# Transposing W2 by DMA instead of on TensorE, with another order of loads and of the first item's work

## The chip, the core and the metric

The kernel runs on one core of one Trainium2 chip. A core has TensorE (PE: matrix products and their weight loads, PEld), VectorE (DVE), ScalarE (ACT), GpSimd (POOL) and SyncE (SP); each runs its own instructions in order. Sixteen DMA engines, which all queues share, move data between HBM (the chip's main memory) and SBUF (the on-chip working memory), and inside SBUF. TensorE writes to PSUM, the accumulator memory, from which VectorE or ScalarE copy to SBUF. The metric is device time in microseconds (us), the median of several runs.

## What is computed

Block-sorted attention with a Sinkhorn-normalised permutation, followed by a layer that takes the larger of two products:

```python
for _ in range(5):                       # P = sort_net, (4 items, 8 heads, 8, 8)
    P = exp(P - max(P)); P = P / sum(P, -1); P = P / sum(P, -2)
k_sorted = einsum('bhij,bhjcd->bhicd', P, k_blocks)      # 8 blocks of 96 rows
v_sorted = einsum('bhij,bhjcd->bhicd', P, v_blocks)
attn = softmax(q_blocks @ k_sorted.T / sqrt(64))         # inside each block
x = (attn @ v_sorted) as (3072 tokens, 512)
out = maximum(x @ w1, x @ w2) @ w_out                    # 512 -> 1024 -> 512
```

q, k and v are (4, 8, 768, 64) in float32; w1 and w2 are 512x1024, w_out is 1024x512.

## The kernel before

**The algebra.** With g = relu(x (W1 - W2)) the output is g Wout + x (W2 Wout). So the kernel overwrites the tile of W1 by W1 - W2 (`w_difference`, L229, in four column pieces `t`), and multiplies W2 by Wout once (`w_product`, L654, four products of eight matmuls into the tile `wc`). For that W2 has to be transposed into `w2T`: `w2_transposes` (L634) does it on TensorE in two batches of 16 matmuls with the identity, each followed by a copy out of PSUM.

**The tiling.** The work goes by batch item `b` = 0 to 3. For each: `sort_k` (three key sorts, `k` in the list below), `sort_v` (four, `v`), `q_transposes` (two, `tq`), `scores` (eight, `SC0` to `SC7`: eight small products and an exponential on ScalarE), `values` (eight, `VA`: eight small products, then a reciprocal and a multiplication on VectorE that make a piece of x), `x_transposes` (four, `tx` or TR: TR`t` takes the results of two `VA`). Then come the `moe_h` units (eight per item, `h` with its token half `ch` and column piece `t`, here split into a first part `a` and a second part `b` for item 0) and twelve `moe_out` units of six products each, which write the result. An h unit reads x transposed by TR0 in its first two products and by TR1 in the next two (for `ch` = 0; TR2 and TR3 for `ch` = 1), and the difference of its column piece.

**What sets the order.** The program is scheduled by hand. Item 0 follows the list `front` (L777): each name is a step, a last letter A or D says that ScalarE or VectorE copies its result out of PSUM, and `F` asks for 512 columns of idle products (`keep_streaming`) ahead of the next scores, values or h part. `diff2` and `diff3` are differences on VectorE; pieces 0 and 1 are made on GpSimd. After it the units of each item run one after the other, and the dictionaries `first_tail`, `second_tail` and `third_tail` (L859 on) say which steps of the next item come after which unit. For item 0 the units 0 to 7 are empty, 8 to 11 are the W2 Wout products, and 12 to 23 the output units; `KS` at 7 is the key sort of item 1, ahead of the products. For items 1 to 3 the units 0 to 7 are h units and 8 to 19 output units.

**Memory that is waited for.** PSUM is one pool of four tiles (`ps`). `load_q(2)` writes into the tile of W2, so W2's readers have to be done. `turn_v` (TURN) rearranges raw v into `v_dc`, from which `sort_v_pair` (VS) reads; four turns cover all of v.

**The queues.** GpSimd issues all loads (float32 in HBM to bfloat16 in SBUF), in program order, with eight in flight. The tiny `seen` copies (L771, L822) hold the queue back: a copy must read its input before the loads behind it are issued. SyncE issues the output writes and, for items 1 to 3, DMA transposes of x (L605) and for items 2 and 3 of q (L419).

```python
    load_w_columns(w2_sb, moe_w2, 2, 4)
    load_w_columns(w1_sb, moe_w1, 2, 4)
    load_w(wo_sb, moe_w_out)
    w_difference(0, nc.gpsimd)
    w_difference(1, nc.gpsimd)
    load_k(1)
```

Of the kernel before, what the change touches and what calls it, by code (L numbers as in the profile page):

```python
# [16 lines left out]
def kernel(  # L17
# [101 lines left out]
    kT = {}  # L119
# [514 lines left out]
    def w2_transposes(t, eng):  # L634
        ps = ps_bf16("tw_ps")
        for n in range(16):
            fb, dmt = t * 4 + n // 4, n % 4
            nc.tensor.matmul(  # L638
                ps[:, n * 128 : (n + 1) * 128],
                w2_sb[:, dmt, fb * 128 : (fb + 1) * 128],  # L640
                ident,
                is_transpose=True,
                start=True,
                stop=True,
            )
        return lambda: evac(
            w2T[:, t * 4 : t * 4 + 4, :].rearrange("p f d -> p (f d)"),
            ps,
            2048,
            two_x=True,  # L650
            eng=eng,
        )
# [109 lines left out]
    for c, n, m in [(2, 2, 0), (4, 3, 1)]:  # L762
# [7 lines left out]
    seen = const.tile([128, 2, 2], BF16, tag="seen", name="seen")  # L770
# [7 lines left out]
        k0A k1D k2A v1A v2D v0A tq0D F0 v3D SC1 SC0 tq1D  # L778
        SC4 F2 VA1 SC5 F1 VA0 SC3 SC2 VA4 tx0D SC7 F3
        VA3 VA2 SC6 tw0D h00a tx1A tw1A VA5 diff3 diff2 h01a h00bA  # L780
        h01bA tx2A h03a VA6 h03bA VA7 h02a h13a tx3D h02bD h12a h13bA
        pe2 h12bD h10a h11a h10bA h11bA
    """.split()
    fills = [0]
# [5 lines left out]
    def front_step(step):  # L790
# [5 lines left out]
        if kind == "F":  # L796
            fills[0] = 512
# [8 lines left out]
        elif kind == "VA":  # L806
            values(0, n[0], fills_due())
        elif kind == "tx":
            x_transposes(0, n[0], eng)
        elif kind == "tw":  # L810
            w2_transposes(n[0], eng)()
        elif kind == "diff":
            w_difference(n[0])
        elif kind == "pe":
            block_diagonals([(0, 2), (0, 3), (1, 1), (1, 2), (1, 3)], 2)
        elif name[-1] == "a":
            moe_h_products(0, n[0], n[1], (0, 2), fills_due())
        else:
            moe_h(0, n[0], n[1], eng, (1, 3))

    front_step(front[0])
    nc.gpsimd.tensor_copy(out=seen[:, 1], in_=kT[0][:, 0:2])  # L822
# [3 lines left out]
    load_w_columns(w1_sb, moe_w1, 1, 2)  # L826
    load_w_columns(w2_sb, moe_w2, 2, 4)
    load_w_columns(w1_sb, moe_w1, 2, 4)
    load_w(wo_sb, moe_w_out)
    w_difference(0, nc.gpsimd)  # L830
    w_difference(1, nc.gpsimd)
    load_k(1)
    for step in front[1:-26]:
        front_step(step)

    load_q(1)
    for piece in range(2):
        for b in (1, 2):
            load_v(b, which=piece)
    load_k(2)  # L840
# [10 lines left out]
    def sorts_and_scores(b):  # L851
# [9 lines left out]
        9: [TQ[0], TURN[0]],  # L861
        10: [SC[0], TQ[1], TURN[1]],
        11: SC[1:4] + TURN[2:4] + [lambda half=half: load_v(3, half=half) for half in range(2)],
        12: VS[0:3],
        13: VS[3:6],
        14: VS[6:8] + [SC[4]],
        15: [VA[0], lambda: pair_q(2, 0)],
        16: [VA[1], lambda: pair_q(2, 1)],
        17: SC[5:8] + [TR[0]],
        18: [VA[2]],  # L870
        19: [VA[3], TR[1]],
        20: [VA[4]],
        21: [VA[5], TR[2]],
        22: [VA[6], VA[7], TR[3]],
# [5 lines left out]
        0: [lambda: q_transposes(2, 0), lambda: q_transposes(2, 1)],  # L880
        2: KS,
        4: SC[0:2],
        5: [VA[0]],
        6: SC[2:4] + [TURN[0]],
        7: [VA[1], TR[0]],
        8: [VA[2], TURN[1]],
        9: [VA[3], TR[1], TURN[2]],
        10: SC[4:7],
        11: [VA[4], TURN[3]],
        12: [VA[5], TR[2], lambda: load_k(3), lambda: load_q(3)],  # L890
        13: [VA[6]],
        14: SC[7:8] + VS[0:2],
        15: [VA[7], TR[3]],
        16: VS[2:4],
        17: [lambda: pair_q(3, 0)],
# [72 lines left out]
```

The softmax here doesn't subtract the row's maximum and nothing guards it: scores larger than these inputs give would overflow.

## Time and profile before

| what | value |
|---|---|
| time, median of 3 runs | 166.6 us (166.55 to 167.2) |
| the profiled execution's own time | 166.83 us |
| its span, first to last instruction | 165.0 us |
| ScalarE exponentials, L556 | 32 of 805 ns |
| x DMA transposes, L605, issue to landing | 12, median 3.8 us (2.8 to 9.5) |
| q DMA transposes, L419, issue to landing | 4, median 5.0 us (4.4 to 5.2) |
| W2 transposes on TensorE, L638 | 32 of 219 ns |
| copies of w2T out of PSUM | VectorE 1.21 us, ScalarE 1.87 us |
| W2 Wout products, L657 | 30 recorded, 379 ns each |
| moved by DMA | 23.90 MB, mean 145 GB/s |

The profile is one execution. Engines overlap, so busy shares do not add up; matmuls are pipelined, so the duration of one (219 ns) is longer than the distance between two. The chain of waits is followed back from the last instruction to whatever released it.

### The profile page before, as it was taken

Reading aid. Unit: us, or ns where it says so; the run is one execution under the profiler, and the core shown is the slowest. Engines: PE = TensorE matmul, PEld = TensorE weight load, DVE = VectorE, ACT = ScalarE, POOL = GpSimd, SP = SyncE. Lnnn points to the kernel's source line nnn. Section 1 sums busy time; section 2 is a strip of 40 time slices with the busy share of each in tenths; the row PEclk is TensorE's granted clock in tenths of the full one; section 3 lists DMA queues with packets and bytes.
Section 4 is the critical chain, followed back from the end, with each engine's and each line's share of the span. In section 5 each row is a group of like instructions: output and inputs, shape, how many; then the busy total and the mean of one; then the engine's idle time right before and its main releaser. Section 6 shows DMA issues by size and latency. Waiting matters only on the chain.

```text
span 165.0 us, 4561 instructions
## 1 busy us (share of the span) xinstructions
PE 157.0 (95%) x2007; PEld 95.4 (58%) x2025; DVE 77.5 (47%) x170; ACT 82.3 (50%) x101; POOL 33.9 (21%) x61
## 2 busy tenths in 40 slices
PE   7889999999999999999999999999999999999992
PEld 7839776756554555557655554575655546654451
DVE  4878995684366564525277763250642420000011
ACT  3489776617239846055652353457447206642020
POOL 7949997131206000000014010000000000000000
PEclk9999999999999999999999999999999999999999
DMA  3999999999999999689515999995025294000333
GB/s 41 204 204 194 164 196 207 209 205 220 210 203 204 220 224 167 175 84 228 111 19 104 126 212 157 200 309 29 0 52 175 50 164 142 0 0 0 127 131 127
DMA packets 30404, 23.90 MB, mean 145 GB/s; under 512 B 16752, under 2 KB 25200, under 8 KB 30384
## 3 DMA queue, kind: packets, MB, share of 16 engines
q0 software_dynamic: 11040, 13.37, 50.0%
q1 hardware_dynamic: 19200, 10.17, 28.9%
q8 instruction: 16, 0.26, 0.7%
q10 hardware_dynamic: 144, 0.07, 0.1%
q14 instruction: 4, 0.03, 0.1%
HBM read 26.75 MB, written 6.29 MB: 200 GB/s over the span
## 4 chain that ended last, share of the span: by engine, by line
PE 81%; DMA 6%; DVE 5%; ACT 3%; POOL 2%; issue 2%
PE out_ps L704 37%; PE h_ps L677 25%; DMA w_sb<-in_moe_w_dram 5%; PE wc_ps L657 4%; PE o_ps L575 4%; PE k_ps L458 3%; PE s_ps L548 3%; ACT e L556 1%; POOL w_sb L189 1%; PE v_ps L523 1%; DMA p_sb<-in_sort_net_dram 1%; PE tq_ps L433 1%; DVE colsum L276 1%; DVE p_sb L273 1%; PE tw_ps L638 1%
## 5 line engine op out<-in xcount | busy, mean ns | idle before, releaser
L704 PE MATMUL out_ps<-wo_sb,g 128*128 128x512 bf16 (+2 forms) x187 | 46.0, 370 | 1.4 <-issue 1.0
L677 PE MATMUL h_ps<-xT,w_sb 128*128 128x384 bf16 x256 | 44.5, 326 | 0.0
L677 PEld LDWEIGHTS <-w_sb 128*128 128x128 bf16 x256 | 24.0, 98 | 15.5
L556 ACT ACTIVATE e<-s_ps 96x768 bf16<-96x768 f32 x32 | 24.0, 805 | 14.8 <-PE s_ps L548 14.8
L691 ACT ACTIVATE g<-h_ps 128x768 bf16<-128x768 f32 x27 | 21.7, 811 | 17.4 <-PE h_ps L677 17.3
L704 PEld LDWEIGHTS <-g 128*128 128x128 bf16 x200 | 17.1, 97 | 15.8
L704 PE MATMUL out_ps<-wc,xT 128*128 128x512 bf16 (+2 forms) x98 | 24.7, 370 | 0.1
L108 ACT COPY o<-out_ps 128x1024 f32<-128x1024 f32 x10 | 10.1, 1012 | 28.0 <-PE out_ps L704 25.2
L592 DVE TENSOR_TENSOR x<-o_ps,rs 96x512 bf16<-96x512 f32 x32 | 22.0, 687 | 1.1
L704 PEld LDWEIGHTS <-xT 128*128 128x128 bf16 x100 | 9.6, 97 | 11.2
L575 PEld LDWEIGHTS <-e 96*128 96x128 bf16 x256 | 11.7, 97 | 5.7 <-DVE v_sb L110 0.2
L586 DVE RECIPROCAL rs<-o_ps 96x8 f32<-96x8 f32 x32 | 6.4, 201 | 17.2 <-PE o_ps L575 17.1
L739 DVE COPY o<-out_ps 128x512 f32<-128x512 f32 (+1 forms) x2 | 1.2, 625 | 27.6 <-PE out_ps L704 27.6
L575 PE MATMUL o_ps<-v_sb,e 96*128 96x65 bf16 x256 | 12.7, 193 | 0.0
L110 DVE CAST kT<-k_ps 128x1024 bf16<-128x1024 f32 x6 | 7.2, 1222 | 8.4 <-PE k_ps L458 8.4
L110 DVE CAST v_sb<-v_ps 96x1024 bf16<-96x1024 f32 x7 | 8.5, 1219 | 4.9 <-PE v_ps L523 2.2
L160 POOL DMA_DIRECT2D v_raw<-in_k_dram x3 | 2.5, 838 | 35.1 <-DVE v_dc L250 31.4
L108 ACT CAST v_sb<-v_ps 96x1024 bf16<-96x1024 f32 x9 | 8.8, 1015 | 1.6 <-PE v_ps L500 0.8
L169 POOL DMA_DIRECT2D v_raw<-in_v_dram x11 | 6.5, 593 | 12.7 <-DVE v_dc L250 6.4
L693 DVE TENSOR_SCALAR g<-h_ps 128x768 bf16<-128x768 f32 x5 | 4.8, 957 | 8.9 <-PE h_ps L677 8.8
L548 PEld LDWEIGHTS <-kT 64*128 64x128 bf16 x256 | 6.1, 94 | 4.8 <-issue 2.6
L548 PE MATMUL s_ps<-qT,kT 64*128 64x96 bf16 x256 | 8.5, 204 | 0.3 <-DVE qT L110 0.2
(97 smaller groups left out, 144.4 us busy)
## 6 DMA issues: line engine op xcount, KB each, us to landing
out_dram<-o SPq DMA_DIRECT2D x11, 512.0 KB, 3.4
v_raw<-in_v_dram POOLq DMA_DIRECT2D x8, 384.0 KB, 13.5
k_raw<-in_k_dram POOLq DMA_DIRECT2D x9, 256.0 KB, 11.0
w_sb<-in_moe_w_dram POOLq DMA_DIRECT2D x4, 256.0 KB, 6.0
w_sb<-in_moe_w_dram POOLq DMA_DIRECT2D x2, 512.0 KB, 9.6
wo_sb<-in_moe_w_out_dram POOLq DMA_DIRECT2D x2, 512.0 KB, 13.7
v_raw<-in_v_dram POOLq DMA_DIRECT2D x3, 256.0 KB, 5.0
q_raw<-in_q_dram POOLq DMA_DIRECT2D x4, 192.0 KB, 9.1
```

The source lines that it names most:

```text
L108: nc.scalar.copy(out=out_ap, in_=in_ap)
L110: nc.vector.tensor_copy(out=out_ap, in_=in_ap)
L169: nc.gpsimd.dma_start(out=v_raw[r0 : r0 + 64, m * n : (m + 1) * n], in_=v_src[b, :, m * n : (m + 1) * n],)
L548: nc.tensor.matmul(ps[:, h2 * 512 + ii * 128 : h2 * 512 + ii * 128 + BLK], kT[b][rows, (hp * 8 + i) * BLK : (hp * 8 + i) * BLK + 128], rhs ...
L556: nc.scalar.activation(out=e[:, 0 : 8 * BLK].rearrange("p (t c r) -> p t c r", t=8, r=R), in_=ps[0:BLK] .rearrange("p (t f) -> p t f", t=8 ...
L575: nc.tensor.matmul(ps[:, h2 * 512 + ii * 65 : h2 * 512 + (ii + 1) * 65], e[:, (h2 * 4 + ii) * BLK : (h2 * 4 + ii) * BLK + 128], v_sb[:, m0 ...
L586: nc.vector.reciprocal(out=rs, in_=ov[:, :, :, 64])
L592: nc.vector.tensor_tensor(out=x, in0=ov[:, :, :, 0:D], in1=rs.to_broadcast([BLK, 2, 4, D]), op=ALU.mult,)
L657: nc.tensor.matmul(ps[:, 0:512], w2T[:, fb, dmt * 128 : (dmt + 1) * 128], wo_sb[:, fb, :], start=(fb == 0), stop=(fb == NFB - 1),)
L677: nc.tensor.matmul(h_ps[ch, t][:, m * 512 : m * 512 + TCH], w1_sb[:, hp, fb * 128 : (fb + 1) * 128], xT[:, b % 2, ch, hp % 2, hp // 2, :], ...
L691: nc.scalar.activation(out=g, in_=src, func=AF.Relu)
L704: nc.tensor.matmul(dst, g_tiles[b, ch, m // 2][:, m % 2, off : off + 128] if m < NFB else xT[:, b % 2, ch, hp % 2, hp // 2, off : off + 12 ...
```

## The change

W2 is transposed by four DMA transposes on SyncE, one for each quarter of its rows, instead of on TensorE; the steps `tw0` and `tw1` and their copies go. In the queue of GpSimd the last half of W1 now goes ahead of the last half of W2; q of item 1 is loaded by pairs of heads, and v of items 1 and 2 in four pieces each instead of two; keys of item 2 are loaded much later; and a third `seen` copy, which reads the last columns that the second transpose writes, stands ahead of q. The first item has another order, with other engines for its copies; a fill asked for while one is pending adds to it. In the first tail q transposes, turns, value sorts, values and x transposes of item 1 come later; in the second the pairing and transposing of item 2's queries move in, and scores, values and x transposes come up to two units later.

```diff
@@ -631,24 +631,10 @@
     w2T = big.tile([128, NFB, DMODEL], BF16, tag="w2T", name="w2T")
     wc = big.tile([128, HP, DMODEL], BF16, tag="wc", name="wc")
 
-    def w2_transposes(t, eng):
-        ps = ps_bf16("tw_ps")
-        for n in range(16):
-            fb, dmt = t * 4 + n // 4, n % 4
-            nc.tensor.matmul(
-                ps[:, n * 128 : (n + 1) * 128],
-                w2_sb[:, dmt, fb * 128 : (fb + 1) * 128],
-                ident,
-                is_transpose=True,
-                start=True,
-                stop=True,
-            )
-        return lambda: evac(
-            w2T[:, t * 4 : t * 4 + 4, :].rearrange("p f d -> p (f d)"),
-            ps,
-            2048,
-            two_x=True,
-            eng=eng,
+    def w2_transposes(dmt):
+        nc.sync.dma_start_transpose(
+            out=w2T[:, :, dmt * 128 : (dmt + 1) * 128],
+            in_=w2_sb[:, dmt, :],
         )
 
     def w_product(dmt):
@@ -767,7 +753,7 @@
     turn_v(first, "A", 36, 56)
     turn_v(first, "A", 56, 80)
     block_diagonals_first()
-    seen = const.tile([128, 2, 2], BF16, tag="seen", name="seen")
+    seen = const.tile([128, 3, 2], BF16, tag="seen", name="seen")
     nc.gpsimd.tensor_copy(out=seen[0:G, 0], in_=p_bf[:, NB - 1, NB - 2 :])
     load_w_columns(w2_sb, moe_w2, 0, 1)
     selections(1)
@@ -775,12 +761,13 @@
     turn_v(first, "D", 80, 96)
 
     front = """
-        k0A k1D k2A v1A v2D v0A tq0D F0 v3D SC1 SC0 tq1D
-        SC4 F2 VA1 SC5 F1 VA0 SC3 SC2 VA4 tx0D SC7 F3
-        VA3 VA2 SC6 tw0D h00a tx1A tw1A VA5 diff3 diff2 h01a h00bA
-        h01bA tx2A h03a VA6 h03bA VA7 h02a h13a tx3D h02bD h12a h13bA
-        pe2 h12bD h10a h11a h10bA h11bA
+        k1A k0A v1D k2A v2A v0D tq0D v3A tq1D SC4 SC5 F2
+        F3 VA4 SC6 SC7 VA5 F0 SC0 VA6 SC1 VA7 F1 SC3
+        tx2D SC2 tx3D VA1 h10a VA0 VA2 h10bA h11a tx0A h11bA diff3
+        VA3 diff2 h13a h01a tx1D h03a h13bD h03bD h01bA h12a pe2 h00a
+        h02a h00bD h02bA h12bA
     """.split()
+
     fills = [0]
 
     def fills_due():
@@ -794,7 +781,7 @@
         kind = name.rstrip("0123456789ab")
         n = [int(x) for x in name if x.isdigit()]
         if kind == "F":
-            fills[0] = 512
+            fills[0] += 512
         elif kind == "k":
             sort_k(0, n[0], 640 if step == front[0] else 0, eng)
         elif kind == "v":
@@ -807,8 +794,6 @@
             values(0, n[0], fills_due())
         elif kind == "tx":
             x_transposes(0, n[0], eng)
-        elif kind == "tw":
-            w2_transposes(n[0], eng)()
         elif kind == "diff":
             w_difference(n[0])
         elif kind == "pe":
@@ -819,25 +804,28 @@
             moe_h(0, n[0], n[1], eng, (1, 3))
 
     front_step(front[0])
-    nc.gpsimd.tensor_copy(out=seen[:, 1], in_=kT[0][:, 0:2])
+    c0 = int(front[0][1]) * 16
+    nc.gpsimd.tensor_copy(out=seen[:, 1], in_=kT[0][:, c0 : c0 + 2])
     load_w_columns(w1_sb, moe_w1, 0, 1)
     load_w_columns(w2_sb, moe_w2, 1, 2)
     selections(3)
     load_w_columns(w1_sb, moe_w1, 1, 2)
+    load_w_columns(w1_sb, moe_w1, 2, 4)
     load_w_columns(w2_sb, moe_w2, 2, 4)
-    load_w_columns(w1_sb, moe_w1, 2, 4)
     load_w(wo_sb, moe_w_out)
+    for dmt in range(HP):
+        w2_transposes(dmt)
     w_difference(0, nc.gpsimd)
     w_difference(1, nc.gpsimd)
     load_k(1)
+    nc.gpsimd.tensor_copy(out=seen[:, 2], in_=w2T[:, NFB - 1, 254:256])
     for step in front[1:-26]:
         front_step(step)
 
-    load_q(1)
-    for piece in range(2):
+    load_q(1, True)
+    for piece in range(4):
         for b in (1, 2):
-            load_v(b, which=piece)
-    load_k(2)
+            load_v(b, 4, which=piece)
 
     for step in front[-26:]:
         front_step(step)
@@ -858,41 +846,39 @@
     TURN = [lambda c=c: turn(both, c) for c in (0, 24, 48, 72)]
     first_tail = {
         7: KS,
-        9: [TQ[0], TURN[0]],
-        10: [SC[0], TQ[1], TURN[1]],
-        11: SC[1:4] + TURN[2:4] + [lambda half=half: load_v(3, half=half) for half in range(2)],
-        12: VS[0:3],
-        13: VS[3:6],
-        14: VS[6:8] + [SC[4]],
-        15: [VA[0], lambda: pair_q(2, 0)],
-        16: [VA[1], lambda: pair_q(2, 1)],
-        17: SC[5:8] + [TR[0]],
-        18: [VA[2]],
-        19: [VA[3], TR[1]],
-        20: [VA[4]],
-        21: [VA[5], TR[2]],
-        22: [VA[6], VA[7], TR[3]],
+        12: [TQ[0]],
+        13: [SC[0], TQ[1]],
+        14: SC[1:4] + TURN[0:2],
+        15: SC[4:5] + TURN[2:4] + [lambda half=half: load_v(3, half=half) for half in range(2)],
+        16: VS[0:3] + [lambda: load_k(2)],
+        17: VS[3:6],
+        18: VS[6:8],
+        19: [VA[0]],
+        20: [VA[1]] + SC[5:8],
+        21: [VA[2], VA[3], TR[0], TR[1]],
+        22: [VA[4], VA[5], TR[2]],
+        23: [VA[6], VA[7], TR[3]],
     }
     SC, VA, TR, KS = sorts_and_scores(2)
     VS = [lambda t=t: sort_v_halved(3, t) for t in range(4)]
     TURN = [lambda c=c: turn(both, c) for c in (0, 24, 48, 72)]
     second_tail = {
-        0: [lambda: q_transposes(2, 0), lambda: q_transposes(2, 1)],
+        0: [lambda: pair_q(2, 0), lambda: pair_q(2, 1)],
+        1: [lambda: q_transposes(2, 0), lambda: q_transposes(2, 1)],
         2: KS,
-        4: SC[0:2],
-        5: [VA[0]],
-        6: SC[2:4] + [TURN[0]],
-        7: [VA[1], TR[0]],
-        8: [VA[2], TURN[1]],
-        9: [VA[3], TR[1], TURN[2]],
+        5: SC[0:2],
+        6: [VA[0], TURN[0]],
+        7: SC[2:4],
+        8: [VA[1], TR[0], TURN[1]],
+        9: [VA[2], TURN[2]],
         10: SC[4:7],
-        11: [VA[4], TURN[3]],
-        12: [VA[5], TR[2], lambda: load_k(3), lambda: load_q(3)],
-        13: [VA[6]],
+        11: [VA[3], TR[1], TURN[3]],
+        12: [VA[4], lambda: load_k(3), lambda: load_q(3)],
+        13: [VA[5], TR[2]],
         14: SC[7:8] + VS[0:2],
-        15: [VA[7], TR[3]],
+        15: [VA[6]],
         16: VS[2:4],
-        17: [lambda: pair_q(3, 0)],
+        17: [VA[7], TR[3], lambda: pair_q(3, 0)],
         18: [lambda: pair_q(3, 1)],
     }
     SC, VA, TR, KS = sorts_and_scores(3)
```

## The prediction, made before the changed kernel ran

> **What bounds the kernel now.** I read the page first, for who is busy, then the chain of waits, for what releases whom, then the GpSimd and VectorE timelines, for when loads land, and the DMA view over three short windows, for what a transpose costs beside a load.
>
> ```profile
> span 165.0 us, 4561 instructions
> ...
> PE 157.0 (95%) x2007; PEld 95.4 (58%) x2025; DVE 77.5 (47%) x170; ACT 82.3 (50%) x101; POOL 33.9 (21%) x61
> ...
> DMA  3999999999999999689515999995025294000333
> ```
>
> Two resources are full: TensorE over the whole span, and the 16 DMA engines over the first 66 us (sixteen slices of 4.1 us). A change can take from one only what the other allows.
>
> ```profile
> 17.03 8.72 DMA w_sb<-in_moe_w_dram
> 25.75 0.05 issue
> 25.80 1.07 PE tw_ps L638 x16
> 26.87 0.24 PE o_ps L575 x8
> ...
> 35.04 3.36 PE h_ps L677 x20
> 38.40 1.64 PE k_ps L458 x96
> 40.03 0.32 PE wc_ps L657
> ```
>
> This is the chain of waits: start, length, what. Until 25.75 it runs through a weight load, afterwards through TensorE almost without a break to the end. The second batch of W2 transposes (`tw_ps`) is what waits for that load. The first item ends at 38.40, the key sort of the second at 40.03, and the W2 Wout products (`wc_ps`) follow.
>
> ```profile
> 28.39 1.29 DVE L231 TENSOR_TENSOR w_sb<-w_sb 128x1024 bf16<-128x1024 bf16 x2 [0.32 <-DMA w_sb<-in_moe_w_dram]
> ```
>
> ```profile
> 35.20 0.58 POOL L160 DMA_DIRECT2D k_raw<-in_k_dram  x1 [0.49 <-DMA k_raw<-in_k_dram]
> 36.52 0.54 POOL L160 DMA_DIRECT2D k_raw<-in_k_dram  x1 [0.74 <-DMA k_raw<-in_k_dram]
> 37.75 0.53 POOL L160 DMA_DIRECT2D k_raw<-in_k_dram  x1 [0.70 <-DMA k_raw<-in_k_dram]
> ```
>
> The last weights are there at 28.3, when VectorE can start the differences W1-W2 of columns 2 and 3. On GpSimd each load waits for the landing of the eighth load before it, so these three waits give the landing of the three thirds of item 1's keys: 34.9, 36.2 and 37.5 (issue at 24.63, 25.2 and 25.75 plus landing times of 10.3, 11.0 and 11.7). TensorE starts the sort at 38.4. The keys arrive with 0.9 us to spare, and Wout just ahead of them at 33.7.
>
> **What the Trainium skill says.** "DMA: Bandwidth & Descriptors", Queues, rings and completion order: each DMA engine goes round the queues that have work, a packet from each in turn, so a transpose issued by SyncE takes slots from the loads of GpSimd. "Advanced Engine Details and Errata", X-Bar Transpose (TRN2): such transposes are said to be as fast as plain transfers, 350 to 400 GB/s. The trace agrees with the first and less with the second. Below are the queues' packets, MB and engine share in three windows: loads alone (30 to 33 us), loads with a transpose and an output (99 to 104), two transposes alone (109.2 to 111).
>
> ```profile
> q0 software_dynamic: 506, 0.63, 120.5%
> ```
>
> ```profile
> q0 software_dynamic: 759, 0.58, 87.3%
> q1 hardware_dynamic: 782, 0.27, 44.9%
> ```
>
> ```profile
> q1 hardware_dynamic: 1978, 0.50, 127.5%
> ```
>
> Alone the loads move 209 GB/s (0.63 MB in 3 us) and the transposes 277. Together they exchange nearly packet for packet, and the loads fall to 116 GB/s. A third place, "TensorE: Matmul & The Clock Gate", PE-mode transpose, says that TensorE's way ends in PSUM and needs a copy after it; here the copies are 1.21 us on VectorE and 1.87 us on ScalarE.
>
> **Part 1, the transposes leave TensorE.** Gone are 2x16 matmuls, 0.90 us per batch (25.80 to 26.70, when the next product starts), and the 0.38 us that TensorE stood idle ahead of the second: 2.2 us at most. The copies were not on the chain.
>
> **Part 2, the new order of item 0.** In the new list everything ahead of `h13a` needs only weight columns 0 and 1. TensorE's part of it: 3 key sorts of 0.55, 4 value sorts of 0.50, 2 q transposes of 0.79, 8 scores of 0.21, 8 values of 0.24, 3 x transposes of 0.34, 4 half units of 0.65 and 4 fills of 0.22, in all 13.3 us from 12.2. Two of waits must be added, as ScalarE first makes five casts (1.0 each, from 12.9) and then eight exponentials of 0.80, so that the last ends near 24.6. TensorE is at `h13a` at about 27.5. That unit needs `diff3`, on VectorE no earlier than 28.39 + 0.65 = 29.05: the bytes ahead of the last weights are the same, so they land at 28.3 again. TensorE waits 1.5 us. From 29.05 on it has twelve half units (7.8), one x transpose (0.34) and the `pe` products (0.25): the front ends at 37.45 instead of 38.40. Of 2.2 us 0.95 is left; the weights took the rest. Moving `w2` behind `w1` in columns 2 to 4 alters nothing, since a difference needs both. The new `seen` copy from key chunk 1 waits for the same cast at 13.95.
>
> **Part 3, four DMA transposes on SyncE.** They need all of W2, so they are issued at 28.4; SyncE has nothing ahead of them. Issue: 1.22 us for x (96x1024) and 2.26 for q (128x1536), some 12 ps an element, so 1.55 for 128x1024; first data at about 29.9. Packets: the q1 queue moves 256-byte packets, so 1024 for each, 4096 in all. Queued against them are the rest of Wout, 3.7 us x 0.205 = 0.76 MB, and the keys, 0.79 MB. The delay D of the keys' last third is unknown. At 116 GB/s throughout, 1.55 MB take 13.3 us, landing at 43.2, D = 5.7. More likely packets alternate, and then the load's packet size decides: 1 KB for a Wout row, 2 KB for a partition's third of keys, 78 and 157 ns of an engine at 209 GB/s. A 256-byte packet adds at least the 15 ns that it takes alone (1978 in 1.8 us over 16 engines), at most what it added in the mixed window: 105 ns for a pair (759 in 5 us), less 59 for a load's 768 bytes, 46. With 15, the two parts take 4.3 and 4.1 us, landing at 38.3, D = 0.8; with 46, 5.8 and 4.9, landing at 40.6, D = 3.1. I take 2.6, nearer the upper, as only a little of the 46 is the output's. The sort cannot use the last third before 40.1 and ends at 40.65, against 40.03 before: **0.6 us lost**, the whole front gain gone. Break-even is D = 2.0; at D below 1.1 the sort ends at 39.1.
>
> By then some 1100 transpose packets are through, one transpose; the other 3000 run alone at 700 to 1000 a microsecond, landing near 41.1, 42.4 and 43.9. The products, 1.74 us each from 40.65, need them at 42.4, 44.1 and 45.9: covered. Without that cover a late transpose costs its lateness.
>
> **Part 4, the gate on GpSimd.** The third `seen` copy (0.18 us) waits for the second transpose. Queued behind it are q of item 1 (now four issues of 0.74), eight pieces of v and q of item 2. Data start at about 42.6; q took 4.9 us and v 7.0 before (37.5 to 42.4 to 49.4), so the last piece is there at 54.5 and the last turn (0.82) done by 55.4. Its reader, `VS` after unit 16, comes at 40.65 + 4x1.74 + 5x1.30 + 2x0.79 + 5x0.21 = 56.7. Covered by 1.3 us; q, wanted at 49, by two. The seven extra issues cost about 4 us of a queue that is 21% busy: nothing.
>
> **Part 5, the tails.** Sorting values and q transposes move four units later, no work added. At the end of the first tail the values crowd: `VA2`, `VA3` and the transposes TR0 and TR1 stand after unit 21 of 23, where TR1 stood at 19.
>
> ```profile
> 70.68 0.69 DVE L592 TENSOR_TENSOR x<-o_ps,rs 96x512 bf16<-96x512 f32 x1
> ```
>
> That is the last x of a pair whose products ended at 69.81: 1.56 us later. A transpose of x in a quiet stretch lands 2.8 us after its issue, one beside loads 5.3 to 9.5. So TR1 lands at least 4.4 us after `VA3`. TensorE reaches its reader, the third product of item 1's first h unit, after units 22 and 23 (2.60), four values (0.98) and two products (0.33): 3.9 us. A wait of 0.5 at least. Loads: q of item 2, v of item 3 and the moved keys of item 2 took 14.8 us (49.4 to 64.2); from 54.5 they end at 69.3, and TR1 is issued near 69. Bounds 0.3 to 3; I take **1.0 us**. The second tail's moves (queries paired a unit later, scores at 5, TR3 at 17 of 19) keep three units or more ahead of each reader: nothing.
>
> **Sum.** +0.6 +1.0 = +1.6 us on the profiled execution's 166.83 us (span 165.0 and 1.83 around it), which is 0.2 over the median of 166.6. On the median: 168.2 us.
>
> **Rivals.**
> - The transposes win the DMA engines (the 116 GB/s of the mixed window holds): keys at 43.2, sort done at 43.75, +3.7, and some 0.7 at TR1: 171.0 us. For it: that window. Against: key packets are larger than its 768 bytes, so lose a smaller share.
> - The other side: the transposes stay out of the keys' way. If D is below 1.1, the sort ends at 39.1, 0.93 sooner; with TR1's wait at its lower 0.3 that is 166.0 us. It decides at D = 2.0 for the sort alone, at 1.7 with that wait. For it: a transpose packet at its 15 ns gives D = 0.8. Against: the mixed window. TensorE can't gain more than 1.1 in any case, since the weights hold the front to 37.45.
> - Values late: if the second transpose lands 2.5 us later than I count, the gate passes it on, `VS` waits 1.3: 169.5 us. For it: DMA engines full to 66 us. Against: the cover.
> - That TensorE's saved work does not shorten anything is part of the forecast: 1.5 of 2.2 us becomes a wait for weights.
>
> **How the numbers follow.** Forecast 0.47, transposes winning 0.18, other side 0.20, values late 0.15. A measurement of this kernel can tell 0.5%, 0.83 us, from none. Faster than 165.8: half of the other side, 0.11. Between 165.8 and 167.4: its other half and the forecast's low end, 0.22. Slower: 0.67. The range leaves out a tenth at each end: 166.0 to 171.0; the forecast's own is 167.0 to 169.4.
>
> **What would show it.** Right: a TensorE wait on VectorE's difference near 27.5 to 29; a front ending at 37.4; key thirds landing at 37 to 40 with a wait ahead of the sort; a wait on the xT transpose at the first h unit of item 1. Wrong: keys landing by 38.5, or products waiting for w2T, which would mean that the transposes, not the keys, are the late side; or a front that ends at 36, if the weights land sooner than 28.

## The result, and the profile after

The changed kernel takes 172.56 us (median of four executions, 170.9 to 174.66) against 166.57 us before: a ratio of 1.0326, 95% interval 1.0239 to 1.0413. It is slower, by 6.0 us, and outside the predicted 166.0 to 171.0. The ratio, unlike the median, leaves out the execution of 174.66 us as a slow one, and is therefore smaller than 172.56 over 166.57. The profiled execution took 170.9 us, 4.1 more than that of before.

The page of the kernel after, the same three rows that were shown of before, and the row of SyncE's DMA queue (packets, MB, share of 16 engines):

```profile
span 168.8 us, 4510 instructions
...
PE 156.0 (92%) x1974; PEld 93.5 (55%) x1993; DVE 75.4 (45%) x169; ACT 80.9 (48%) x100; POOL 37.5 (22%) x69
...
DMA  3999999999999999999606899994025253000333
...
q1 hardware_dynamic: 23424, 11.22, 31.5%
```

TensorE has 1.0 us less work in a span 3.8 us longer. The DMA engines are full to the end of the 19th slice of 4.2 us, some 80 us, where before they first fell back at 66. SyncE's queue has 4224 packets more than before (19200), 4096 of them W2's.

The chain of waits of the kernel after (start, length, what), in the stretch where before it ran through TensorE almost without a break:

```profile
17.50 9.55 DMA w_sb<-in_moe_w_dram
...
28.54 10.00 DMA w2T<-w_sb
38.54 0.05 issue
38.59 0.19 POOL seen L821
...
38.83 2.80 POOL q_raw L143 x4
41.62 13.61 DMA v_raw<-in_v_dram x2
...
55.26 0.83 DVE v_dc L250
...
56.13 0.88 PE v_ps L523 x48
...
69.38 5.50 DMA xT<-x
74.87 0.04 issue
74.91 3.73 PE h_ps L663 x22
```

From 17.5 to 55.3 the end of the program hangs on transfers and their issue: weights, a W2 transpose, the gate (the third `seen` copy), q and v. TensorE comes into the chain only at 56.1, and leaves it again for a transpose of x.

TensorE's timeline after (start, time from first to last instruction, group, and in brackets the idle time before it and what ended it) shows where it stands:

```profile
36.49 1.71 PE L458 MATMUL k_ps<-bd,k_raw 64*64 64x64 bf16 x96
38.13 7.08 PE L643 MATMUL wc_ps<-wo_sb,w2T 128*128 128x512 bf16 x31
...
56.13 0.88 PE L523 MATMUL v_ps<-bd,v_dc 64*128 64x64 bf16 x48 [1.27 <-DVE v_dc L250]
...
65.56 0.34 PE L548 MATMUL s_ps<-qT,kT 64*128 64x96 bf16 x8 [0.57 <-DVE x L592]
...
74.29 4.35 PE L663 MATMUL h_ps<-xT,w_sb 128*128 128x384 bf16 x24 [2.94 <-DMA xT<-x]
```

The same two places in TensorE's timeline before:

```profile
38.33 1.71 PE L458 MATMUL k_ps<-bd,k_raw 64*64 64x64 bf16 x96
...
70.94 4.06 PE L677 MATMUL h_ps<-xT,w_sb 128*128 128x384 bf16 x24
```

The key sort starts at 36.49 with no wait, 1.84 us ahead of before (38.33), and the products follow without a wait for W2's transposes. Then come three waits that before did not have: 1.27 for values, 0.57 for a PSUM tile, 2.94 for xT (and 0.13 more inside that group). The first h unit of item 1 begins at 74.29 instead of 70.94, and TensorE ends at 165.39 instead of 161.92. The sum: -1.84 +1.27 +0.57 +3.07 is +3.07, against +3.47 measured; 0.4 us is spread over small shifts.

SyncE's queue shows the transposes' cost from the side of their issue:

```profile
27.13 11.52 SPq L635 DMA_TRANSPOSE w2T<-w_sb  x4
54.68 9.37 SPq L710 DMA_DIRECT2D out_dram<-o  x2
65.53 8.00 SPq L605 DMA_TRANSPOSE xT<-x  x3
```

The x transpose issued at 65.53 (TR0) landed at 74.16, that of 69.38 (TR1) at 74.87. Beside them ran the keys of item 2, landing at 69.84, 71.67 and 73.45, and an output until 73.51. Before, the loads had ended by then.

The remaining 1.7 us between the profiled execution and the median go with TensorE's clock. The four executions had spans of 168.8, 170.2, 170.7 and 172.5 us, at mean granted clocks of 0.999, 0.99, 0.99 and 0.98. A mean of 0.99 over 170 us is 3.4 us at half clock, or 1.7 us of lost work. Only the first of the four was profiled, so where the others lost it is not shown.

### The profile page after: what moved, and what is told of

It is laid out like the page before. It is cut to its first block, busy times and chain, and to the rows that moved or that the text cites. A ratio compares the mean times of both kernels' runs of the same rounds, so it can differ in the third digit from the quotient of the medians.

```text
span 168.8 us, 4510 instructions
## 1 busy us (share of the span) xinstructions
PE 156.0 (92%) x1974; PEld 93.5 (55%) x1993; DVE 75.4 (45%) x169; ACT 80.9 (48%) x100; POOL 37.5 (22%) x69
## 4 chain that ended last, share of the span: by engine, by line
PE 60%; DMA 24%; DVE 6%; POOL 4%; issue 2%; ACT 1%; SPq 1%
PE out_ps L690 31%; PE h_ps L663 19%; DMA v_raw<-in_v_dram 8%; DMA w2T<-w_sb 6%; DMA w_sb<-in_moe_w_dram 6%; DMA xT<-x 3%; PE o_ps L575 3%; PE k_ps L458 2%; PE s_ps L548 2%; POOL w_sb L189 2%; POOL q_raw L143 2%; PE v_ps L523 1%; DVE x L592 1%; DMA p_sb<-in_sort_net_dram 1%; SPq L635 1%
## 5 line engine op out<-in xcount | busy, mean ns | idle before, releaser
L663 PE MATMUL h_ps<-xT,w_sb 128*128 128x384 bf16 x256 | 44.3, 326 | 3.1 <-DMA xT<-x 2.9
L575 PEld LDWEIGHTS <-e 96*128 96x128 bf16 x256 | 11.1, 97 | 6.1 <-ACT e L556 0.9
L110 DVE CAST kT<-k_ps 128x1024 bf16<-128x1024 f32 x5 | 5.9, 1219 | 10.2 <-PE k_ps L458 10.2
L169 POOL DMA_DIRECT2D v_raw<-in_v_dram x15 | 8.0, 558 | 9.0 <-DVE v_dc L250 6.5
```

What stands on the lines that cost most here:

```text
L110: nc.vector.tensor_copy(out=out_ap, in_=in_ap)
L169: nc.gpsimd.dma_start(out=v_raw[r0 : r0 + 64, m * n : (m + 1) * n], in_=v_src[b, :, m * n : (m + 1) * n],)
L575: nc.tensor.matmul(ps[:, h2 * 512 + ii * 65 : h2 * 512 + (ii + 1) * 65], e[:, (h2 * 4 + ii) * BLK : (h2 * 4 + ii) * BLK + 128], v_sb[:, m0 ...
L663: nc.tensor.matmul(h_ps[ch, t][:, m * 512 : m * 512 + TCH], w1_sb[:, hp, fb * 128 : (fb + 1) * 128], xT[:, b % 2, ch, hp % 2, hp // 2, :], ...
```

## The experiments

In the expectations A is the theory that a run tries and B its rival, each as that text gives them. In most, A is that each new wait comes from one meeting of late loads with a reader or an x transpose, and goes when they are kept apart. Three letters mean the same throughout: C, the clock is lowered after long waits; D, the megabyte of W2 transposes costs DMA time by itself; E, the place of one load decides. Ratios are against the kernel before, run beside each.

### The values of item 3 out of the way of the x transposes

```diff
-        15: SC[4:5] + TURN[2:4] + [lambda half=half: load_v(3, half=half) for half in range(2)],
+        15: SC[4:5] + TURN[2:4],
...
-        0: [lambda: pair_q(2, 0), lambda: pair_q(2, 1)],
+        0: [lambda: pair_q(2, 0), lambda: pair_q(2, 1), lambda: nc.gpsimd.tensor_copy(out=seen[:, 3], in_=xT[:, 1, 0, 1, 1, TCH - 2 : TCH])]
+        + [lambda half=half: load_v(3, half=half) for half in range(2)],
```

> The changed kernel, but v of item 3 is held back until the second x transpose of item 1 has landed. Theory A (the two x transposes land 8.6 and 5.5 us after issue because loads of q, v and k share the DMA engines with them): without v in front of them the loads are done near 66 us, the wait ahead of the first h unit of item 1 falls from 3.1 us to at most 1.2, and the span from 168.8 to about 166.8. Rival B (the transposes simply stand too late in the tail, loads or not): the wait stays near 3 us and the span near 168.8. Theory C (the waits of TensorE cost it its clock in some executions): with A, the granted clock of all executions is 0.999 and their times lie within 0.5% of each other; without C they scatter as before (168.8 to 172.5).

178.32 us, ratio 1.0732 (1.0679 to 1.0784). TR0 took 3.4 us instead of 8.6, and TR1 2.8. TensorE's timeline of this run:

```profile
71.54 3.74 PE L663 MATMUL h_ps<-xT,w_sb 128*128 128x384 bf16 x22 [0.51 <-DMA xT<-x]
...
85.74 2.72 PE L663 MATMUL h_ps<-xT,w_sb 128*128 128x384 bf16 x8 [7.09 <-DMA xT<-x]
```

The wait of 2.94 fell to 0.51, so it did come from loads beside TR0 and TR1. But now the loads met TR3, which took 13.3 us (72.44 to 85.70), and its reader waited 7.09. A was right on the cause and wrong on the time. The same run's windows (us, then busy time of each engine, granted clock, DMA share, GB/s) show a second price:

```profile
83.00:86.00 3.00, 0.26 (x1) 0.10 (x1) 0.00 (x0) 0.00 (x0) 0.00 (x0) 0.50 1.19 184
86.00:89.00 3.00, 3.00 (x11) 1.47 (x10) 0.00 (x0) 0.81 (x1) 0.00 (x0) 0.50 0.86 167
89.00:92.00 3.00, 3.00 (x38) 1.75 (x37) 0.02 (x1) 1.94 (x3) 0.00 (x0) 0.91 0.00 0
```

The clock stays at half for 3.8 us after TensorE has work again (85.74 to 89.5): eight h products take 2.72 us there, where 22 took 3.74 before, so each takes twice as long.

### W2 on TensorE, in the new order of everything else

```diff
-        VA3 diff2 h13a h01a tx1D h03a h13bD h03bD h01bA h12a pe2 h00a
+        VA3 diff2 tw0A h13a h01a tx1D h03a h13bD h03bD h01bA tw1A h12a pe2 h00a
...
-    for dmt in range(HP):
-        w2_transposes(dmt)
-    nc.gpsimd.tensor_copy(out=seen[:, 2], in_=w2T[:, NFB - 1, 254:256])
```

(and `w2_transposes` as it was before).

> The changed kernel, but W2 is transposed on TensorE in two batches at the end of item 0, without the DMA transposes and without the copy on GpSimd that waits for them; everything else as changed. Theory A (the 1 MB of transposes and the gate behind them push q and v back by 5 to 6 us): v of items 1 and 2 has landed by 50 us, no wait ahead of the value sorts, the x transposes of item 1 find idle DMA engines and the wait ahead of the first h unit is at most 1.2 us; TensorE works 1.8 us more in front; span 166.5 to 167. Rival B (the moved tails alone cost the time): the waits stay, span 170 or more. The keys' last third should land 9.2 us after the last weights, as before the change, against 9.9 with the transposes beside them.

172.52 us, ratio 1.0372 (1.0309 to 1.0435). With no DMA transposes of W2 the time is that of the changed kernel. The values landed at 49.2 and `VS` had no wait; the x transposes were late all the same. GpSimd's timeline and then TensorE's:

```profile
54.88 0.55 POOL L169 DMA_DIRECT2D v_raw<-in_v_dram  x1 [9.80 <-DVE v_dc L250]
56.35 1.55 POOL L169 DMA_DIRECT2D v_raw<-in_v_dram  x3 [0.93 <-DVE v_dc L250]
57.87 1.67 POOL L160 DMA_DIRECT2D k_raw<-in_k_dram  x3
```

```profile
74.72 2.72 PE L677 MATMUL h_ps<-xT,w_sb 128*128 128x384 bf16 x8 [2.20 <-DMA xT<-x]
```

The values of item 3 wait 9.8 us for the turns, which the new tail has moved to units 14 and 15; the keys of item 2 are queued behind them. The DMA engines move 33 GB/s from 51 to 53 us and nothing from 53 to 55, and what they could have moved then is moved beside TR0 (7.9 us). The clock was at half from 74.38 to 77.79. I had expected a wait of at most 1.2; the new order of everything else is a cost of its own.

### W2 by DMA transposes, in the old order of everything else

```diff
-        VA3 VA2 SC6 tw0D h00a tx1A tw1A VA5 diff3 diff2 h01a h00bA
+        VA3 VA2 SC6 h00a tx1A VA5 diff3 diff2 h01a h00bA
...
+    for dmt in range(HP):
+        w2_transposes(dmt)
+    nc.gpsimd.tensor_copy(out=seen[:, 2], in_=w2T[:, NFB - 1, 254:256])
```

> The kernel before with the one edit that W2 is turned by the four DMA transposes, with the copy on GpSimd ahead of q of item 1; order of item 0, weights, tails and all later loads as before the change. Theory D (the 1 MB of transposes is paid on the DMA engines by everything loaded after them, whatever the order of the tails): q of item 1 lands near 46 us and v of items 1 and 2 near 54, TensorE waits 1 to 2 us for q and 4 to 6 us for v ahead of the value sorts, with half a clock for 3.4 to 6.8 us after it: 172 to 175 us. Rival B (the reordered tails are what costs, the transposes are harmless): 166 to 168 us.

174.35 us, ratio 1.0475 (1.0443 to 1.0507). TensorE's timeline:

```profile
40.08 0.69 PE L458 MATMUL k_ps<-bd,k_raw 64*64 64x64 bf16 x32 [0.81 <-DMA k_raw<-in_k_dram]
...
48.73 0.86 PE L433 MATMUL tq_ps<-ident,q_raw 128*64 128x128 bf16 x24 [4.40 <-DMA q_raw<-in_q_dram]
```

D was right, and larger than expected: in the old tail q is wanted at 44.3 and lands at 48.7, and the clock was at half for 3.41 us after; v, for which 4 to 6 us were expected, was not waited for. So each half of the change alone costs 6 to 8 us, and together they cost no more, because the new tail's later `TQ`, `TURN` and `VS` stand where the delayed q and v arrive (the next run puts that to the test). Within the half without the transposes, the order of item 0, that of the weights and the second tail were not run apart.

### The new order with the old first tail; the new order without the gate

```diff
-        12: [TQ[0]],
-        13: [SC[0], TQ[1]],
...
+        9: [TQ[0], TURN[0]],
+        10: [SC[0], TQ[1], TURN[1]],
...
```

> The changed kernel with the first tail of the kernel before (its steps of item 1 four units earlier; keys of item 2 still loaded late). Theory A (the later tail is an answer to q and v landing 4 and 6 us later): TensorE waits for q at its first transposes (about 1 us) and for v at the value sorts (4 to 6 us), the x transposes no longer cost anything; span 169 to 171. Rival B (the later tail is itself what costs, since it puts the x transposes next to their reader): span 166 or less.

174.03 us, ratio 1.0461 (1.0416 to 1.0506). TensorE's timeline:

```profile
44.15 0.53 PE L433 MATMUL tq_ps<-ident,q_raw 128*64 128x128 bf16 x12 [1.24 <-DMA q_raw<-in_q_dram]
...
57.14 1.46 PE L523 MATMUL v_ps<-bd,v_dc 64*128 64x64 bf16 x48 [3.78 <-DVE v_dc L250]
```

The waits move back to q and v, and the xT wait is gone. A was right on the waits: the new tail is needed by the late loads, and its price is the crowd at its end. The profiled span, 173.3, is beyond the 171 that A allowed; the clock was at half for 6.83 us after the wait for v.

```diff
-    nc.gpsimd.tensor_copy(out=seen[:, 2], in_=w2T[:, NFB - 1, 254:256])
```

> The changed kernel without the GpSimd copy that holds q of item 1 back until the second transpose has landed. Theory A (a transpose gets one 256-byte packet for each load packet, so beside loads it crawls at about 100 packets a us): q and v follow the keys without a gap, the last of them near 50 us, but the third and fourth transpose land after 46 us, and TensorE waits 3 us or more for w2T ahead of the W2 Wout products; span 170 or more. Rival B (the gate only costs): w2T is there in time all the same, the 1.3 us ahead of the value sorts goes, span 167.5 or less.

187.91 us, ratio 1.129 (1.1227 to 1.1353). TensorE's timeline:

```profile
54.66 3.59 PE L643 MATMUL wc_ps<-wo_sb,w2T 128*128 128x512 bf16 x8 [11.45 <-DMA w2T<-w_sb]
```

A was right here, beyond its size. With q and v let in beside them the second to fourth W2 transposes landed at 54.6 to 58.4 instead of 38.5 to 41.7. The gate is not a cost that could be saved; the transposes hardly moved beside the loads.

### One load moved ahead of another, without and with the W2 transposes

The keys of item 2 go right behind its queries instead of behind the values of item 3, in the kernel with W2 on TensorE, and in the changed kernel:

```diff
+    load_k(2)
...
-        16: VS[0:3] + [lambda: load_k(2)],
+        16: VS[0:3],
```

> The changed order with W2 transposed on TensorE, as run earlier, and keys of item 2 loaded right behind q of item 2 instead of behind v of item 3. There the DMA engines stood idle at 49 to 55 us, as v of item 3 has to wait for the later turns and the keys stood behind it. Theory E (in that run it is this queue order, not the amount of data, that puts loads beside the x transposes of item 1): keys land near 57 us, v of item 3 near 64, the x transposes of item 1 within 4 us of their issue, the wait of 2.2 us and the 3.4 us of half clock go: 168.5 to 169.5 us instead of 172.5. Rival: the transposes still take over 6 us: 172 us.

> The changed kernel with the same one move: keys of item 2 ahead of v of item 3. Theory D (here the DMA engines have no idle time before 73 us, so the order of the two does not matter, and v's packets are three times as long as those of the keys): the x transposes of item 1 land as late or later, the wait ahead of the first h unit is 3 us or more: 172 to 174 us. Theory E (queue order): the wait falls to 1 us, 169 to 170 us.

With W2 on TensorE it took 168.65 us, ratio 1.0148 (1.0122 to 1.0173): 3.9 us less for one line, and the fastest of all variants. TR0 landed in 5.1 us, TR1 in 2.8, and the wait is down from 2.20:

```profile
73.39 2.92 PE L677 MATMUL h_ps<-xT,w_sb 128*128 128x384 bf16 x17 [0.55 <-DMA xT<-x]
```

The clock was full in every execution. Of the 2.5 us that are left against the kernel before, the key sort's later start (38.83) is 0.5, and waits of 0.57 for a PSUM tile and 0.55 for xT are 1.1; the rest was not looked into. With the DMA transposes it took 171.99 us, ratio 1.0342 (1.0299 to 1.0385): no gain, TR0 8.5 us, the wait 2.84. There the idle stretch that the keys fill in the other kernel does not exist: the transposes' megabyte, with q and v held back behind it, has taken it. E holds without them, D with them.

### The loads spread further

Three kernels keep the transposes and move more. The first loads keys 2 behind queries 2, holds the values of item 3 until the queries of item 2 are transposed, and turns them later; the second also brings the first tail's scores, sorts and x transposes up by a unit; the third loads q and k of item 3 ahead of those values and turns and sorts the values in the third tail. The second and third extract show each run against the one before it, and not its whole edit:

```diff
+    load_k(2)
...
+        + [lambda: nc.gpsimd.tensor_copy(out=seen[:, 3], in_=qT[2][:, HP - 1, R - 1, 126:128])]
+        + [lambda half=half: load_v(3, half=half) for half in range(2)]
+        + [lambda: load_q(3)],
```

```diff
-        20: [VA[1]] + SC[5:8],
-        21: [VA[2], VA[3], TR[0], TR[1]],
...
+        19: [VA[0], VA[1]],
+        20: [VA[2], VA[3], TR[0], TR[1]],
```

```diff
-        + [lambda half=half: load_v(3, half=half) for half in range(2)]
-        + [lambda: load_q(3)],
+        + [lambda: load_q(3), lambda: load_k(3)]
+        + [lambda half=half: load_v(3, half=half) for half in range(2)],
```

> The changed kernel with keys of item 2 loaded right behind its q, and v of item 3 held back until all DMA transposes of x of item 1 and of q of item 2 have landed; q of item 3 goes to a buffer of its own behind that v, and the four turns of item 3's v stand up to four units later. Theory A (transposes are late only where loads run beside them): all four x transposes of item 1 land 2.8 to 4 us after their issue, the waits ahead of the h units are 0.5 to 1.2 us in the first half and none in the second, the granted clock is 0.99 or more in all executions, and the time is 168 to 169 us. Rival B (v of item 3, now loaded from 80 us on, comes too late for its turns or delays the x transposes of item 2): a new wait of over 1 us after 88 us, 170 us or more.

> The loads as in the run before, and the first tail in another order: the last scores stand ahead of the value sorts, where TensorE waits for v, the sorts begin a unit later, and the first two x transposes stand one unit earlier. Theory A: the wait ahead of the value sorts (1.3 us) and that ahead of the first h unit (3.1 us) are both under 0.3 us, what is left is the 1.6 to 1.8 us by which the first item ends sooner: 164.5 to 165.5 us, less than the kernel before, with a clock of 0.999. Rival B (the late v of item 3 costs elsewhere): 166.5 or more.

> An attempt at a faster version on the basis of the run with both loads and tail changed: q and keys of item 3 are loaded into buffers that are free by then (those of q and keys of item 1), ahead of v of item 3, whose turns and sorts move into the third tail; the value sorts of item 1 stand three, three and two after units 17, 18 and 19. Theory A (all that is left of the loss is loads that meet a reader): no wait of over 0.7 us after 40 us, 165 to 166.5 us against 166.1 to 166.6. Rival B (v of item 3 or x transposes of item 2 are late again): a wait of over 1 us between 95 and 120 us, 168 us or more.

172.76, 171.55 and 169.21 us, ratios 1.0406 (1.0355 to 1.0457), 1.0298 (1.0259 to 1.0338) and 1.0174 (1.0145 to 1.0204). The wait ahead of item 1's first h unit is 0.51 us in the first and gone in the others. It comes back an item later: in the first as 1.94 at 98.7 (values) and 1.91 at 109.3 (xT, a transpose of 14.4 us), in the second as 1.42 and 1.06, in the third as 1.24 and 1.48. TensorE's timeline of the third:

```profile
104.50 0.50 PE L659 MATMUL h_ps<-xT,w_sb 128*128 128x384 bf16 x2 [1.24 <-DMA xT<-x]
106.48 1.78 PE L659 MATMUL h_ps<-xT,w_sb 128*128 128x384 bf16 x10 [1.48 <-DMA xT<-x]
```

B was right for the time. What the third gains, it gains by splitting one long wait into short ones; its clock was full. None of the three is faster than the kernel before.

### Work for TensorE during the wait

Twelve products on zeros, whose result is overwritten, fill the wait ahead of item 1's first h unit:

```diff
-        units = [lambda ch=ch, t=t: moe_h(b, ch, t) for ch in range(2) for t in range(4)]
+        units = [
+            lambda ch=ch, t=t: moe_h(b, ch, t, n=6144 if (b, ch, t) == (1, 0, 0) else 0)
...
```

> The changed kernel with twelve products of 512 columns on zeros (2.6 us of TensorE, their results overwritten) ahead of the first h unit of item 1, where TensorE waits 3.1 us for the x transposes. Theory C (an idle TensorE of 2 us or more loses half its clock for 3.4 us in some executions, which is what the runs beyond the profiled one lost): the fills lie in the wait, the clock is 0.998 or more in all executions and the times all lie at 170 to 171.5 us. Rival (the scatter comes from the DMA alone): the times scatter over 170.5 to 174 as before, or rise by the 2.6 us.

171.21 us, ratio 1.0299 (1.0268 to 1.033), with six of seven executions between 170.84 and 171.87, and clocks of 0.997 or more in all seven. The seventh, 173.84 us, is the profiled one. TensorE's timeline:

```profile
58.77 0.88 PE L523 MATMUL v_ps<-bd,v_dc 64*128 64x64 bf16 x48 [2.44 <-DVE v_dc L250]
...
73.84 2.75 PE L82 MATMUL h_ps<-fill 128*128 128x512 bf16 x12
77.26 0.49 PE L663 MATMUL h_ps<-xT,w_sb 128*128 128x384 bf16 x2 [0.67 <-DMA xT<-x]
```

The wait is as long as ever, 3.42 us from 73.84 to 77.26, but now it is mostly filled. C is right on the clock: three of four executions were at 0.98 or 0.99 without the fills, none with them. What that is worth is less certain: 1.35 us by the two medians, but 0.0027, or 0.4 us, by the two ratios, whose intervals overlap. And the rival holds for the seventh execution, which is late at a full clock, with 2.44 us of waiting for values where the changed kernel's profile has 1.27.

### Shorter load packets

Values of item 3 in eight pieces per half, packets of 1.5 KB for 6 KB, on top of the changed kernel with keys 2 moved up:

```diff
-        15: SC[4:5] + TURN[2:4] + [lambda half=half: load_v(3, half=half) for half in range(2)],
+        15: SC[4:5] + TURN[2:4] + [lambda half=half: load_v(3, 8, half=half) for half in range(2)],
```

> The changed kernel with the keys of item 2 right behind its queries (as in e10_k2_early), and the values of item 3 loaded in eight pieces per half, so that a packet of them is 1,536 bytes instead of 6,144; the same bytes. Theory 'one transpose packet per load packet': the x transposes beside these loads get more turns; TR0 lands at most 6.5 us after its issue instead of 8.5, the wait ahead of the first h unit falls from 2.8 to at most 1.8 us, and the time is 170 to 171 us. Rival 'only the bytes queued ahead matter': TR0 still takes 8 us or more, the wait stays at 2.8 to 3.1 us, and the time is about 172 us.

177.59 us, ratio 1.0565 (1.0488 to 1.0641): both theories missed. TR0 took 7.8 us. TensorE's timeline, and then the queues (packets, MB, share) from 70 to 76 us:

```profile
74.52 0.48 PE L663 MATMUL h_ps<-xT,w_sb 128*128 128x384 bf16 x2 [2.09 <-DMA xT<-x]
79.12 5.72 PE L663 MATMUL h_ps<-xT,w_sb 128*128 128x384 bf16 x22 [4.12 <-DMA xT<-x]
```

```profile
q0 software_dynamic: 547, 0.67, 96.6%
q1 hardware_dynamic: 807, 0.20, 40.4%
```

The transposes got more turns, 135 packets a microsecond, but the loads fell to 112 GB/s and lasted until 81.3 instead of 73, so that TR1 was late in its turn (79.08). The sixteen pieces also wait on GpSimd for the landing of the eighth load before each. The run says that short packets are no remedy; it does not separate packet size from the longer queue.

## Why the prediction was wrong, by its steps

**Part 1, right.** The transposes left TensorE, and nothing waited for their copies. With W2 on TensorE in the new order the key sort began 10.92 us after the last weights (27.91 to 38.83), without it 9.45, so 1.5 of the 2.2 us "at most" show there.

**Part 2, right.** The front ends 9.45 us after the last weights land (27.04 to 36.49 here; 28.20 to 37.65 with the old tail; 28.66 to 38.11 without the gate); predicted were 9.15 (28.3 to 37.45). Only the landing itself came earlier in the profiled execution than the 28.3 that I carried over; it spreads from 27.0 to 28.7 over the runs. So the expected wait of 1.5 us for a difference is absent from that execution, and the front ends near 36, as foreseen for weights sooner than 28. With later weights the wait is there, 1.60 us without the gate and 0.97 with the old tail:

```profile
29.05 1.47 PE L663 MATMUL h_ps<-xT,w_sb 128*128 128x384 bf16 x8 [0.97 <-DVE w_sb L231]
```

**Part 3, right mechanism, mis-sized.** D was taken as 2.6 us. The keys' last third landed 9.89 us after the last weights, against 9.17 before: D is 0.7, at the lower bound. Over the other runs with this front it is 0.3 to 1.5 (9.47 to 10.70). With the transposes in the old order it is 2.7 (11.90): there W2 is loaded ahead of the last of W1, and the transposes start at 25.78, 2.4 us before the last weights land. So the order of the weights, said to alter nothing, decides when the transposes start. The queues of the kernel after (packets, MB, share) from 31 to 35 us, keys beside W2:

```profile
q0 software_dynamic: 416, 0.73, 97.4%
q1 hardware_dynamic: 366, 0.09, 17.1%
```

and from 37 to 39, W2 alone:

```profile
q1 hardware_dynamic: 2120, 0.53, 127.0%
```

A load packet of 1755 bytes on average took 4 x 16 / 416 = 154 ns of an engine, and would take 134 at the 209 GB/s of loads alone. A transpose packet thus added some 23 ns (20 for each 0.88 of them), nearer the 15 that it takes alone than the 46 of the mixed window, in which an output ran too. Instead of 0.6 us lost at the sort, 1.84 were gained; 1.26 of them are luck, as the weights landed at 27.04 and not at 28.30. With weights at 28.20 and 28.66 the sort began at 37.65 and 38.11, 0.7 and 0.2 us sooner than before. So the rival of the other side was right here (D below 1.1) and the kernel was slower all the same; the transposes winning, the other rival, is out; and the values were late, for another reason than that rival gave.

**Part 4, right mechanism, cover mis-sized.** The gate opened at 38.59, not 41.1, but q then shared the engines with two transposes and the last piece of v landed at 55.23, not 54.5:

```profile
55.26 0.82 DVE L250 COPY v_dc<-v_raw 128x768 uint32<-128x768 uint32 x1 [1.55 <-DMA v_raw<-in_v_dram]
```

TensorE was 2.5 us ahead of the forecast at the end of the sort (38.13, not 40.65), lost 0.7 of that on the way, and reached `VS` at 54.86 instead of 56.7. Of 1.3 us cover, 1.84 went to the earlier reader and 0.7 to the later turn: 1.3 - 1.84 - 0.7 = -1.24, and the wait is 1.27. Here the gain ahead of the transfer was paid back at its reader; the prediction worked out the cover from the forecast alone and never from the rival's earlier sort. The size belongs to this execution: in the five other profiled runs with the same steps up to `VS` the wait was 0.45 to 2.44 us, and there an earlier sort did not mean a longer wait: the shortest follows the earliest sort (36.66), the longest the latest (37.96), as weights, gate and v move together. That the rival with late values had also named 1.3 us is chance: its second transpose came 2.5 us later than counted, the measured one 2.5 us sooner.

**Part 5, the step that failed.** It priced the wait at item 1's first h unit at 1.0 us (bounds 0.3 to 3), from TR1 alone and with the loads ending at 69.3; it was 3.07. TR1 was issued at 69.38, as foreseen. But the loads ended at 73.45: behind the last piece of v they took 18.2 us (from 55.2), not the 14.8 carried over from before (from 49.4). The engines moved 220 GB/s in both stretches, but 4.04 MB instead of 3.26, and 0.68 of the 0.78 MB more are SyncE's queue, writes of the output above all. So TR1 took 5.5 us, and TR0, issued at 65.53 and not in the sum, 8.6. Either would have held TensorE without the other: TR0 landed 2.8 us after TensorE was free (71.36), TR1 3.2 us after it could have come to the third product (71.69). The prediction had the numbers: 5.3 to 9.5 us beside loads, from 65.5, is 70.8 to 75.0. The first experiment shows that it was the loads beside TR0 and TR1, and the two runs with W2 on TensorE that the place of one load is enough to cause the wait.

**The first tail's scores, moved at no price, had one.** `SC[5:8]` now stand in the unit of `VA1`, whose PSUM tile they need: 0.57 us. Before, there was a unit between them.

**Missing: the clock.** No term for what a wait does to the work after it, some 1.7 us of the median by the granted clocks.

Term by term, forecast and then measured in the profiled execution: the sort +0.6 and -1.84, values 0 and +1.27, scores 0 and +0.57, xT +1.0 and +3.07.

## What to carry to other kernels

Where the DMA engines were full, a transfer added there shifted what stood behind it, and the cost showed at later readers (4.40 us for q in the old tail, 2.94 for xT in the new one), not beside the new transfer. So list each transfer up to where the engines fall idle, with its reader, and work out the cover anew for every rival. DMA transposes were the weak side beside loads (8.6 us instead of 2.8), so keep those with a near reader in stretches without loads, and order the loads by when they can be issued, so that none that waits holds up one that could go. Price a wait of TensorE of two microseconds or more with the clock that it may cost afterwards, 1.7 us for each 3.41 at half.

## What the runs showed of the hardware

Packets of a DMA transpose (256 bytes) got through much more slowly beside loads: 1060 a microsecond alone (2120 in 2 us), 91 beside key loads (366 in 4), and 91 again with the values of item 3 beside transposes of x and q in the first experiment, from 75 to 85 us:

```profile
q0 software_dynamic: 312, 1.52, 81.7%
q1 hardware_dynamic: 910, 0.23, 20.9%
```

Here three transpose packets go to one load packet of 4.9 KB on average; beside the key loads (1.75 KB) it was 0.9 to one, and beside the short packets of the last experiment (1.2 KB) 1.5 to one, at 135 a microsecond. So the packets that the profile counts are not exchanged one for one, as the prediction had it after "DMA: Bandwidth & Descriptors", Queues, rings and completion order. Nor does that page say so: each engine finishes a whole packet of one queue before it turns to the next, but a packet there is a group of descriptors, typically 9 to 17, and no run here shows how such groups lie in the profile's packets. An x transpose (96x1024, 768 packets) at 91 a microsecond would take 8.4 us; TR0 took 8.6. Without loads one took 2.8 us; the longest of all took 17 (87.46 to 104.45 in the last of the spread kernels). Why the rate is 91, no run settles.

The Trainium skill, "TensorE: Matmul & The Clock Gate", Part 1, puts the return to half clock after an idle window of about 3.4 us that runs freely. The runs agree with the length of the step: the stretches at half clock were 3.41 or 6.83 us, and 13.65 after the 11.45 us without the gate. They came after shorter waits, too: 2.20 us (W2 on TensorE), 2.23 (a second wait without the gate), 2.84 (keys moved up); the 2.94 of the profiled execution of the changed kernel and the 2.44 of the one with fills brought none. In these profiled executions no wait of under 2 us was followed by one.
